# Loading K of head 0 ahead of the first wq and wo pieces in a one-token attention and MLP training step

## The chip, the cores and the metric

The kernel runs on one core of one Trainium2 chip. The metric is the device time of one execution in microseconds (us), the median of several runs. Each experiment is compared with runs of before taken in the same session, so the number for before differs a little from place to place (402.67 to 403.04). The start times in us come from the one profiled run of each kernel.

Names are those of the profile: PE is TensorE (PEld its weight loads), DVE VectorE, ACT ScalarE, POOL GpSimd, SP SyncE, and L288 is line 288 of the kernel. K0 and V0 are K and V of head 0.

## The reference, cut to what matters

One token `x` (640 wide) attends over a cache of 32 heads, each with K and V of 4096 x 128 in bf16. A small MLP runs beside it, a sigmoid gate mixes the two, and all gradients are returned, among them dK and dV, as large as the caches.

```python
x = A_x
g = _sigmoid((x * gate_w).sum(-1, keepdims=True))
a = _A_ref(x, A_k_cache, A_v_cache, A_wq, A_wo)   # softmax(q k^T) v, then @ wo
b = _B_ref(x, B_w1, B_b1, B_w2)
return g * a + (1 - g) * b
# ... and the vjp of this with grad_out
```

K and V are 67 MB together, and as much again is written as dK and dV, plus the weights and their gradients. Each byte is used for little arithmetic.

## The kernel before: the parts that matter

The bulk loads go out on the SyncE (SP) queue, in program order. Three small loads of 1.2 KB each (`vec_rows`: the rows of x, grad_out and the gate weights) go out on the ACT queue.

```python
    nc.scalar.dma_start(vec_rows[0:RC, :], x_rows)                 # L109
    nc.scalar.dma_start(vec_rows[RC:2 * RC, :], dy_rows)           # L110, grad_out
    nc.scalar.dma_start(vec_rows[2 * RC:3 * RC, :], gw_rows)       # L111, gate_w
    # ... load_k, load_v, load_wq, load_wo: one nc.sync.dma_start each
    load_wq(0)      # 1280 KB
    load_wo(0)      #  640 KB
    load_k(0)       # 1024 KB
    load_v(0)
    load_k(1)
    load_v(1)
    load_wo(1)
    # ... w1, b1, load_k(2), load_v(2), w2
```

Before the first head, a chain prepares its query and its output gradient. It starts from `vec_rows` (gate, then `da_bc`), multiplies `wo` with `da_bc` (L288, four passes), projects `x` through `wq` (L278), and ends in `x_ps` (L320). Only after these in PE's program order come the first transposes of K0:

```python
    prep_steps(0, 0)                 # qcol (wq), do_part (wo), ..., x2 -> x_ps
    for _ in range(8):
        slot(0, 9, 9)
    tk = []
    for c in range(NT):
        k_chunk(0, c, tk)            # transposes of K0 (L587)
    # ...
    for h in range(H):
        # ...
        load_k(h + 3)                # 4 K and 4 V buffers: load_k(4) waits for head 0's
        load_v(h + 3)                # last matmuls on K0 (L720)
        # ...
        period(h)
```

The loads through K3 and V3 need no buffer to come free. The load of K4 is the first that waits for compute.

Of the kernel before, what the change touches and what calls it, by code (L numbers as in the profile page):

```python
# [16 lines left out]
def kernel(  # L17
# [100 lines left out]
    def load_k(h):  # L118
        if h < H:
            kts[h] = kv_in.tile([P, J, Dh], BF16, name="Kn", tag="Kn", bufs=KB)  # L120
            nc.sync.dma_start(kts[h][:], Kv[h])

    def load_v(h):
        if h < H:
            vts[h] = kv_in.tile([P, J, Dh], BF16, name="Vn", tag="Vn", bufs=VB)
            nc.sync.dma_start(vts[h][:], Vv[h])

    def load_wq(w):
        if w < H // WG:
            wqs[w] = wts.tile([P, RC, WG * Dh], BF16, name="wq_g", tag="wq_g")  # L130
            nc.sync.dma_start(wqs[w][:], wq_v[:, :, w * WG * Dh:(w + 1) * WG * Dh])

    def load_wo(g):
        if g < NG:
            wos[g] = wts.tile([P, G, D], BF16, name="wo_g", tag="wo_g", bufs=3)
            nc.sync.dma_start(wos[g][:], wo_v[g])
# [3 lines left out]
    def load_w2(c):  # L140
        a, b = CH[c][0], min(CH[c][1], FM)
        w2cs[c] = mlp.tile([P, 5, D], BF16, name="w2c", tag="w2c", bufs=2)
        nc.sync.dma_start(w2cs[c][:, 0:b - a, :], w2_v[:, a:b, :])

    load_wq(0)
    load_wo(0)
    load_k(0)
    load_v(0)
    load_k(1)
    load_v(1)  # L150
# [711 lines left out]
```

## Time and profile before

| what | before | where it is read |
|---|---|---|
| time | 403.04 us, median of 3 runs (402.11 to 404.58) | the runs |
| span of the profiled run | 400.6 us | page, head |
| bytes moved by DMA | 164.93 MB | page, part 2 |
| rate in most slices | 415 to 428 GB/s | page, part 2 |
| busy: DVE, PE, PEld, ACT | 76%, 74%, 67%, 44% | page, part 1 |
| first transpose of K0 | 17.07 us | timeline |

These lines are part 2 of the page of before: the span in 40 equal slices of about 10 us, with the busy share of the 16 DMA engines in tenths and the rate that they moved.

```profile
DMA  8999999999999999999999999999999999999995
GB/s 288 420 415 397 421 426 417 418 423 422 425 419 424 421 422 419 419 424 422 427 415 426 422 423 419 418 428 422 421 424 423 422 421 417 423 422 416 425 378 232
DMA packets 28360, 164.93 MB, mean 412 GB/s; under 512 B 3260, under 2 KB 3964, under 8 KB 12556
```

The DMA engines are full from the second slice to the 38th. The Trainium skill, "Perfetto Trace Analysis", section Identifying the Most-Contended Engine, advises judging DMA by the HBM rate, not by occupancy. Here both say the same: about 421 GB/s in the middle, where that page (section Engine Utilization) puts the ceiling of one core's 16 engines at about 435. This trace agrees: 421 is 3% below that ceiling.

The second reading is of the start. This is the timeline of before: start in us, busy us, engine, line, operation, count, and in brackets the idle time before it with what ended it.

```profile
0.73 0.45 SPq L131 DMA_DIRECT2D wq_g<-in_A_wq_dram  x1
1.24 0.51 SPq L136 DMA_DIRECT2D wo_g<-in_A_wo_dram  x1
1.80 0.42 SPq L121 DMA_DIRECT2D Kn<-in_A_k_cache_dram  x1
...
7.04 0.17 PE L189 MATMUL cols_ps<-ident_bf,vec_rows 15*128 15x15 bf16 x1 [7.04 <-DMA vec_rows<-in_gate_w_dram]
7.09 0.33 SPq L136 DMA_DIRECT2D wo_g<-in_A_wo_dram  x1
...
11.09 0.43 ACT L229 COPY da_bc<-dab_ps 128x320 f32<-128x320 f32 x1 [2.09 <-PE dab_ps L104]
...
11.54 0.82 DVE L288 SCALAR_TENSOR_TENSOR junk<-wo_g,da_bc 128x640 bf16<-128x640 bf16 x1 [1.14 <-ACT da_bc L229]
...
17.05 0.17 PE L320 MATMUL x_ps<-m,sel 128*128 128x16 bf16 x1 [0.26 <-DVE m L315]
17.07 1.95 PE L587 MATMUL tr<-ident_f,Kn 128*128 128x128 f32 x8
```

The first transpose of K0 follows `x_ps` at once. No wait for K0 stands before it. The wait that heads the chain is the one for `vec_rows`.

### The profile page before, as it was taken

Reading aid. Unit: us, or ns where it says so; the run is one execution under the profiler, and the core shown is the slowest. Engines: PE = TensorE matmul, PEld = TensorE weight load, DVE = VectorE, ACT = ScalarE, POOL = GpSimd, SP = SyncE. Lnnn points to the kernel's source line nnn. Section 1 sums busy time; section 2 is a strip of 40 time slices with the busy share of each in tenths; the row PEclk is TensorE's granted clock in tenths of the full one; section 3 lists DMA queues with packets and bytes.
Section 4 is the critical chain, followed back from the end, with each engine's and each line's share of the span. In section 5 each row is a group of like instructions: output and inputs, shape, how many; then the busy total and the mean of one; then the engine's idle time right before and its main releaser. Section 6 shows DMA issues by size and latency. Waiting matters only on the chain.

```text
span 400.6 us, 13611 instructions
## 1 busy us (share of the span) xinstructions
PE 296.6 (74%) x5872; PEld 268.1 (67%) x5872; DVE 303.5 (76%) x791; ACT 177.1 (44%) x411; POOL 47.2 (12%) x94
## 2 busy tenths in 40 slices
PE   0688898778888788778885988819887888888200
PEld 0588787668777678668875878718776777777200
DVE  2438766646799999856688799837999997899850
ACT  1355555324554455325543555605545455545000
POOL 0001101021110111211110113101110121111000
PEclk9999999959999999959998899977999999999655
DMA  8999999999999999999999999999999999999995
GB/s 288 420 415 397 421 426 417 418 423 422 425 419 424 421 422 419 419 424 422 427 415 426 422 423 419 418 428 422 421 424 423 422 421 417 423 422 416 425 378 232
DMA packets 28360, 164.93 MB, mean 412 GB/s; under 512 B 3260, under 2 KB 3964, under 8 KB 12556
## 3 DMA queue, kind: packets, MB, share of 16 engines
q1 hardware_dynamic: 17136, 93.41, 56.5%
q0 software_dynamic: 11104, 70.64, 42.3%
q8 instruction: 46, 0.75, 0.7%
q14 instruction: 14, 0.11, 0.1%
q10 hardware_dynamic: 60, 0.01, 0.0%
HBM read 82.03 MB, written 82.03 MB: 410 GB/s over the span
## 4 chain that ended last, share of the span: by engine, by line
DVE 36%; DMA 34%; PE 17%; issue 5%; ACT 4%; SPq 0%; POOL 0%; ACTq 0%; POOLq 0%
DMA Kn<-in_A_k_cache_dram 29%; DVE dK_sb L612 9%; DVE dV_sb L612 8%; PE tr L587 7%; DVE junk L385 4%; DMA out_dram<-wo_g 4%; ACT tT L589 4%; PE sA L667 3%; DVE junk L288 3%; PE sA L596 2%; PE sB L720 2%; DVE junk L537 2%; DMA vec_rows<-in_gate_w_dram 1%; DVE wo_g L374 1%; DVE dj L707 1%
## 5 line engine op out<-in xcount | busy, mean ns | idle before, releaser
L589 ACT COPY tT<-tr 128x512 f32<-128x512 f32 x256 | 142.3, 588 | 133.9 <-PE tr L587 133.1
L596 PEld LDWEIGHTS <-tT 128*128 128x128 bf16 x2048 | 79.8, 98 | 40.1 <-ACT tT L589 34.6
L587 PE MATMUL tr<-ident_f,Kn 128*128 128x128 f32 x512 | 82.0, 298 | 9.7 <-DMA Kn<-in_A_k_cache_dram 9.7
L612 DVE TENSOR_TENSOR dV_sb<-p_bf,qd 128x2048 bf16<-128x2048 bf16 x64 | 78.0, 1218 | 0.2 <-issue 0.2
L612 DVE TENSOR_TENSOR dK_sb<-ds_bf,qd 128x2048 bf16<-128x2048 bf16 x64 | 77.7, 1216 | 0.0
L587 PE MATMUL tr<-ident_f,Vn 128*128 128x128 f32 x512 | 72.5, 277 | 0.0
L587 PEld LDWEIGHTS tr<-ident_f,Kn 128*128 128x128 f32 x512 | 61.2, 152 | 11.2 <-issue 11.2
L596 PE MATMUL sA<-qd,tT 128*128 128x48 bf16 x1024 | 48.8, 187 | 23.7 <-ACT dq_all L725 12.7
L587 PEld LDWEIGHTS tr<-ident_f,Vn 128*128 128x128 f32 x512 | 55.9, 141 | 0.0
L596 PE MATMUL sB<-qd,tT 128*128 128x48 bf16 x1024 | 46.1, 183 | 0.0
L667 PEld LDWEIGHTS <-Vn 128*128 128x128 bf16 x1024 | 30.2, 95 | 10.4 <-issue 10.4
L667 PE MATMUL sA<-e_bf,Vn 128*128 128x48 bf16 x1024 | 30.7, 183 | 7.7 <-DVE zs L687 6.1
L629 POOL DMA_DIRECT2D out_dram<-dK_sb x30 | 17.3, 576 | 138.6 <-DVE rz L689 90.6
L720 PE MATMUL sB<-ds_bf,Kn 128*128 128x48 bf16 x1024 | 32.1, 185 | 1.4 <-DVE ds_bf L709 1.4
L671 DVE TENSOR_REDUCE m<-sA 128x1 f32<-128x32 f32 x32 | 6.1, 189 | 35.2 <-PE sA L596 28.5
L720 PEld LDWEIGHTS <-Kn 128*128 128x128 bf16 x1024 | 29.4, 97 | 1.6 <-issue 1.6
L642 POOL DMA_DIRECT2D out_dram<-dV_sb x26 | 14.1, 544 | 136.8 <-DVE o_all L712 50.0
L288 DVE SCALAR_TENSOR_TENSOR junk<-wo_g,da_bc 128x640 bf16<-128x640 bf16 x32 | 26.3, 821 | 2.6 <-ACT da_bc L229 1.1
L385 DVE SCALAR_TENSOR_TENSOR junk<-wq_g,dq_bc 128x1024 bf16<-128x1024 bf16 (+1 forms) x25 | 25.1, 1005 | 0.2
L707 DVE TENSOR_SCALAR_CACHE_REDUCE dj<-sB,rz 128x128 f32<-128x128 f32 x32 | 11.1, 346 | 9.2 <-PE sB L701 9.2
L691 ACT ACTIVATE p_bf<-e_bf,rz 128x64 bf16<-128x64 bf16 x32 | 11.1, 348 | 13.6 <-DVE rz L689 10.7
L698 DVE SCALAR_TENSOR_TENSOR pj<-sB,e_bf 128x32 f32<-128x32 f32 x32 | 6.1, 190 | 12.5 <-PE sB L596 12.4
(152 smaller groups left out, 275.5 us busy)
## 6 DMA issues: line engine op xcount, KB each, us to landing
Kn<-in_A_k_cache_dram SPq DMA_DIRECT2D x32, 1024.0 KB, 23.1
Vn<-in_A_v_cache_dram SPq DMA_DIRECT2D x32, 1024.0 KB, 27.5
out_dram<-dK_sb POOLq DMA_DIRECT2D x30, 1024.0 KB, 11.7
out_dram<-dV_sb POOLq DMA_DIRECT2D x26, 1024.0 KB, 11.8
wq_g<-in_A_wq_dram SPq DMA_DIRECT2D x4, 1280.0 KB, 23.7
wo_g<-in_A_wo_dram SPq DMA_DIRECT2D x8, 640.0 KB, 16.7
out_dram<-wo_g POOLq DMA_DIRECT2D x7, 640.0 KB, 12.2
out_dram<-dwq_t SPq DMA_DIRECT2D x4, 896.0 KB, 18.3
```

The lines of the kernel that those rows point to most:

```text
L288: nc.vector.scalar_tensor_tensor(junk[:, 0:D], in0=wos[g][:, i, :], scalar=1.0, in1=da_bc[:], op0=ALU.mult, op1=ALU.mult, accum_out=gp["do ...
L385: nc.vector.scalar_tensor_tensor(junk[:, c0:c1], in0=wqs[w][:, rc, c0:c1], scalar=1.0, in1=dq_bc[:, w * WG * Dh + c0:w * WG * Dh + c1], op ...
L587: nc.tensor.transpose(tp[:, t, :], flat[:, k * P:(k + 1) * P], ident_f[:])
L589: nc.scalar.copy(sb[:].rearrange("p a b -> p (a b)"), tp[:].rearrange("p a b -> p (a b)"))
L596: nc.tensor.matmul(out[:, 2 * k:2 * k + W], lhsT=tb[:, t, par, :], rhs=vec[:, par, :].unsqueeze(1).to_broadcast([P, W // 2, 2]), start=(pa ...
L612: nc.vector.tensor_tensor(dst[:, a:b, :].rearrange("p j (a b) -> p j a b", b=2), col[:, a:b, :].unsqueeze(2).to_broadcast([P, n, Dh // 2, 2]),
L629: ring(h).dma_start(dKv[h], st["dK"][:])
L642: ring(h).dma_start(dVv[h], st["dV"][:])
L667: nc.tensor.matmul(O, lhsT=vts[h][:, j, :], rhs=st["e"][:, j:j + 1].to_broadcast([P, W]), start=(j == 0), stop=(j == J - 1))
L691: nc.scalar.activation(p_bf[:], e[:].unsqueeze(2).to_broadcast([P, J, 2]), ACT.Copy, scale=rz[:])
L707: nc.vector.tensor_scalar(dj[:], PT, rz[:], None, ALU.mult, ALU.add, accum_out=dd[:])
L720: nc.tensor.matmul(DQ, lhsT=kts[h][:, j, :], rhs=ds[:, j, 0:1].to_broadcast([P, W]), start=(j == 0), stop=(j == J - 1))
```

## The change

The intent is to have the first head's K in place earlier by loading it before the weights. Nothing else moves: the instruction streams of PE, DVE, ACT and POOL are in the same order in both kernels.

```diff
+    load_k(0)
     load_wq(0)
     load_wo(0)
-    load_k(0)
     load_v(0)
     load_k(1)
     load_v(1)
```

## The prediction

> **What bounds the kernel now.** The 16 DMA engines. The slice table shows DMA at 9 tenths in every slice but the first (8) and the last (5), and 415 to 428 GB/s in nearly every slice from the second to the 38th; 164.93 MB move in a 400.6 us span. No compute engine is near that: DVE 76%, PE 74%, PEld 67%, ACT 44%. At 421 GB/s the bytes alone need about 392 us (an estimate from those numbers), so only some 9 us are start and tail. This agrees with the Trainium skill, "Perfetto Trace Analysis", section Engine Utilization, which gives about 435 GB/s for 16 DMA engines as one core's ceiling.
>
> **What the change does.** It adds and removes nothing. On the SyncE queue the first three issues become K0, wq, wo instead of wq, wo, K0 (1024, 1280 and 640 KB); the instruction order on the other engines is identical. Whatever comes fourth starts at the same byte count.
>
> **Does the start wait for K0?** No. The chain of waits in 0 to 18 us reads: vec_rows (three small ACT-queue loads) lands at 6.9; gate and broadcasts until da_bc at 11.5; four L288 passes over wo to 15.0; d_ps, qd, dc_ps, m, x_ps to 17.2; only then, in PE program order, the first transposes of K0. K0 issues at 1.80 us and takes about 9.6 to land (11.4), over 5 us before its first use. Landing earlier buys nothing.
>
> **Does it hurt wq and wo?** From stretches of 2 us, 1.05 MB have moved by about 6.4 us, 2.36 MB by 8.8 and 3.01 MB by 10.4. So (estimates) K0 lands near 6.5, wq near 9 and wo near 10.5 to 11; they are needed at 11.3 (qcol) and 11.5 (L288). It just fits.
>
> **The side effect I expect.** vec_rows heads the chain. In the DMA packet records the grad_out and gate_w rows move only when wq is nearly drained, and wq's landing (it frees the wo(1) issue at 7.1) nearly coincides with gate_w's (6.9). With K0 and wq in front of gate_w it should land later: about 50 KB more per DMA engine at about 26 GB/s, so 1.5 us later (estimate, 0 to 2). The first K0 transpose would move from 17.1 to about 18.6 us. If grad_out and gate_w slip in behind K0 alone, the start gains up to 1 us.
>
> **How much is critical.** Almost nothing. The loads through head 3's V (14.8 MB) do not wait for compute, and only about 11 MB have moved by 30 us, when the first wait on a K buffer (L720) ends. That leaves some 8 us of backlog, so a 1.5 us later start of compute keeps the DMA engines full. PE and DVE have slack, and at about 50 to 82 us the chain waits on a K load anyway, which absorbs the lag. What remains is jitter in the tail (last two slices, 378 and 232 GB/s).
>
> **Prediction.** 403.2 us, 8 in 10 between 401.4 and 405.0. Faster by over 2%: 1.5%; within 2%: 97%; slower by over 2%: 1.5%.
>
> **What would show it.** Right: slices from the second on still about 420 GB/s; K0 landing near 6.5 us; first K0 transpose within 2 us of 17.1, released by x_ps and not by the K0 load; span within 2 us. Wrong at a step: qcol or L288 waiting on wq or wo; vec_rows landing by 6.9; a middle slice below 410 GB/s.
>
> **What would make it wrong.** The shifted completion order changing when later SyncE issues are released, so that the queue runs dry; a phase shift between loads and stores changing the tail by several us; wo landing much later than estimated; vec_rows starving for many us.

## The result, and the profile after

The changed kernel took 403.06 us (median of 6 runs, 402.36 to 404.16), before took 402.96 us (6 runs, 402.11 to 404.58). The ratio is 1.0003, with a 95% interval of 0.998 to 1.0027: the same. A ratio is the mean time of one kernel's fast runs over that of the other's of the same rounds, so it is not quite the ratio of the medians quoted.

Part 2 of the page of the changed kernel, the same lines as above:

```profile
DMA  7999999999999999999999999999999999999985
GB/s 276 422 415 404 419 425 421 419 420 423 423 421 424 421 423 417 418 426 421 422 422 422 424 425 418 418 423 421 424 423 423 425 422 420 424 418 420 425 361 215
DMA packets 28360, 164.93 MB, mean 411 GB/s; under 512 B 3260, under 2 KB 3964, under 8 KB 12556
```

The DMA picture is unchanged from the second slice to the 38th; the last two are a little lower (361 and 215 for 378 and 232). The timeline of the changed kernel's start:

```profile
0.73 0.39 SPq L121 DMA_DIRECT2D Kn<-in_A_k_cache_dram  x1
1.18 0.42 SPq L131 DMA_DIRECT2D wq_g<-in_A_wq_dram  x1
1.65 0.52 SPq L136 DMA_DIRECT2D wo_g<-in_A_wo_dram  x1
...
5.65 0.33 SPq L136 DMA_DIRECT2D wo_g<-in_A_wo_dram  x1
...
6.20 0.17 PE L189 MATMUL cols_ps<-ident_bf,vec_rows 15*128 15x15 bf16 x1 [6.20 <-DMA vec_rows<-in_gate_w_dram]
...
10.25 0.42 ACT L229 COPY da_bc<-dab_ps 128x320 f32<-128x320 f32 x1 [2.09 <-PE dab_ps L104]
...
11.48 0.82 DVE L288 SCALAR_TENSOR_TENSOR junk<-wo_g,da_bc 128x640 bf16<-128x640 bf16 x1 [1.92 <-DMA wo_g<-in_A_wo_dram]
...
16.99 0.17 PE L320 MATMUL x_ps<-m,sel 128*128 128x16 bf16 x1 [0.26 <-DVE m L315]
17.01 1.95 PE L587 MATMUL tr<-ident_f,Kn 128*128 128x128 f32 x8
```

K0 is in by about 5.6 us: the profile's waits of the SyncE queue put the issue of the second wo piece, at 5.65, behind K0's landing, as they put it behind wq's, at 7.09, before. But K0 is read first at 17.01, against 17.07 before. So it lies unused for over 11 us. Two things on the chain changed and nearly cancelled: `vec_rows` came 0.84 us earlier in this run (6.20 for 7.04), and wo, now last of the three, came so late that L288 waits for it (1.92 us idle, ended by the wo load) where it had waited for `da_bc`.

This cancelling leaves two explanations for a total that did not move. They differ in what a microsecond at the start is worth, so the experiments vary the start.

### The profile page after: what moved, and what is told of

Read it like the earlier page. It is cut to its first block, busy times and chain, and to the rows that moved or that the text cites. A ratio compares the mean times of both kernels' runs of the same rounds, so it can differ in the third digit from the quotient of the medians.

```text
span 401.4 us, 13611 instructions
## 1 busy us (share of the span) xinstructions
PE 295.7 (74%) x5872; PEld 267.4 (67%) x5872; DVE 303.5 (76%) x791; ACT 177.1 (44%) x411; POOL 47.0 (12%) x94
## 4 chain that ended last, share of the span: by engine, by line
DVE 36%; DMA 33%; PE 20%; ACT 4%; issue 2%; SPq 0%; ACTq 0%; DVEq 0%
DMA Kn<-in_A_k_cache_dram 31%; DVE dV_sb L612 9%; PE tr L587 8%; DVE dK_sb L612 8%; DVE junk L385 5%; ACT tT L589 4%; PE sA L667 3%; DVE junk L288 3%; PE sA L596 3%; DMA wo_g<-in_A_wo_dram 2%; PE sB L720 2%; DVE junk L537 2%; DVE wo_g L374 1%; DVE junk L494 1%; DVE dj L707 1%
## 5 line engine op out<-in xcount | busy, mean ns | idle before, releaser
L667 PEld LDWEIGHTS <-Vn 128*128 128x128 bf16 x1024 | 30.2, 96 | 10.5 <-issue 10.5
L288 DVE SCALAR_TENSOR_TENSOR junk<-wo_g,da_bc 128x640 bf16<-128x640 bf16 x32 | 26.3, 821 | 2.5 <-DMA wo_g<-in_A_wo_dram 1.9
## 6 DMA issues: line engine op xcount, KB each, us to landing
out_dram<-dK_sb POOLq DMA_DIRECT2D x30, 1024.0 KB, 11.4
out_dram<-wo_g POOLq DMA_DIRECT2D x7, 640.0 KB, 11.8
```

Source lines behind the costliest of these rows:

```text
L288: nc.vector.scalar_tensor_tensor(junk[:, 0:D], in0=wos[g][:, i, :], scalar=1.0, in1=da_bc[:], op0=ALU.mult, op1=ALU.mult, accum_out=gp["do ...
L667: nc.tensor.matmul(O, lhsT=vts[h][:, j, :], rhs=st["e"][:, j:j + 1].to_broadcast([P, W]), start=(j == 0), stop=(j == J - 1))
```

## The experiments

**Theory A.** The 16 DMA engines bound the kernel. The loads that need no compute (through K3 and V3) are a backlog that keeps them full until about 37 us (an estimate from their 14.8 MB and the rates), so the start of compute may move within some microseconds and cost or gain nothing.

**Theory B.** The start chain counts one for one, and the change was neutral only because an earlier `vec_rows` and a later wo cancelled.

**Rival C**, to the first half of A: the chain of compute and waits bounds the kernel, as the page's chain view may suggest (DVE 36%, DMA 34%, PE 17% for before).

### e1_pool_rows: the small rows on another queue (a miss as a test)

```diff
-    nc.scalar.dma_start(vec_rows[RC:2 * RC, :], dy_rows)
-    nc.scalar.dma_start(vec_rows[2 * RC:3 * RC, :], gw_rows)
+    nc.gpsimd.dma_start(vec_rows[RC:2 * RC, :], dy_rows)
+    nc.gpsimd.dma_start(vec_rows[2 * RC:3 * RC, :], gw_rows)
```

> Before's load order, but the grad_out and gate_w rows go out on the GpSimd queue instead of the ACT queue, ahead of everything else there. All theories: vec_rows lands by about 4 us instead of 6.9, so the first K0 transpose comes at 14 to 15 us instead of 17.1. Theory A (the DMA backlog absorbs the start): total within 0.3% of before (402 to 404 us). Theory B (the start chain counts one for one, and the change was neutral only because an earlier vec_rows and a later wo cancelled): 2 to 3 us less, about 400.3 us.

The total was 402.81 us (6 runs) against 402.67; ratio 0.9999 (0.9981 to 1.0018). But the premise failed: the rows were not early. PE had them at 8.0 us, later than before, and the first K0 transpose came at 17.98. So as a test of an earlier start it says nothing. It is one more point: a start 0.9 us later, with no cost that these runs resolve.

### e2_k_wo_wq: wo ahead of wq (a miss as a test)

```diff
-    load_wq(0)
-    load_wo(0)
     load_k(0)
+    load_wo(0)
+    load_wq(0)
```

> K0, wo, wq: as the change, with wo ahead of wq, so that wo (640 KB) is no longer the last of the three. L288 should start when da_bc is ready (10.3 to 10.7 us) and no longer wait for wo; qcol may now wait for wq until about 11.3, which is off the chain. First K0 transpose about 0.8 us earlier than in the changed kernel, at 16.1 to 16.3 us. Theory A: total within 0.3% of before. Theory B: about 0.8 us less than before, at the edge of what five rounds resolve.

Ratio 0.9997 (0.9977 to 1.0017), 402.74 us (5 runs). L288 no longer waited for wo, as expected, but `vec_rows` landed at 6.9 in this run, so `da_bc` came later and the first transpose came at 16.96, not at 16.1 to 16.3. The two theories were not told apart by this.

### e3_rows_after_v0 and e4_rows_after_v1: the start made later, in two doses

```diff
-    nc.scalar.dma_start(vec_rows[0:RC, :], x_rows)      # and the other two
     load_wq(0)
     load_wo(0)
     load_k(0)
     load_v(0)
+    nc.sync.dma_start(vec_rows[0:RC, :], x_rows)        # and the other two: e3 here,
     load_k(1)
     load_v(1)
+                                                        # e4 here instead
     load_wo(1)
```

> Before's order, with the three vec_rows loads on the SyncE queue behind V0. They land with V0, at about 4.0 MB moved, 10 to 11 us, so the first K0 transpose comes at 20 to 21 us, 3 to 4 us later than before. Theory A: within 0.3% of before. Theory B: 3 to 4 us more, about 406.5 us.

> Before's order, with the three vec_rows loads on the SyncE queue behind V1. They land at about 6.2 MB moved, 15 to 18 us; first K0 transpose 25 to 28 us, so head 0 frees its K buffer at about 38 to 41 us, where the loads that need no compute (14.8 MB) run out at about 37. Theory A: 1 to 6 us more than before, and the GB/s of the slice at 30 to 40 us below 400. Theory B: the full delay, 8 to 11 us more, about 413 us.

The first K0 transposes of e3 and of e4:

```profile
24.14 1.95 PE L587 MATMUL tr<-ident_f,Kn 128*128 128x128 f32 x8
```

```profile
28.84 1.95 PE L587 MATMUL tr<-ident_f,Kn 128*128 128x128 f32 x8
```

In e3 the delay was twice what I had expected: the first K0 transpose came at 24.14 us, 7.1 us later than before's 17.07. The total was 403.54 us (6 runs), ratio 1.0018 (0.9998 to 1.0038): about 0.7 us for 7.1 us of delay, and not clear of zero. Theory B asked for 7.

In e4 the first transpose came at 28.84 us, 11.8 us later than before, and the total was 408.34 us (4 runs), ratio 1.0137 (1.0111 to 1.0164), which is 5.5 us more. Part 2 of the page of e4 shows where it went:

```profile
DMA  8998799999999999999999999999999999999995
GB/s 294 419 416 329 267 416 414 422 425 422 418 415 422 424 421 419 419 424 422 422 423 423 422 423 421 416 425 424 422 420 427 422 421 422 413 421 419 424 396 228
```

The fourth and fifth slice fell to 329 and 267 GB/s. The stretches view of e4 (start and end in us, length, busy time of the engines, then the granted clock, the busy share of the DMA engines, and GB/s) resolves this:

```profile
35.00:37.00 2.00, 1.88 (x36) 1.69 (x35) 0.52 (x3) 1.97 (x5) 0.00 (x0) 1.00 1.01 418
37.00:39.00 2.00, 1.71 (x45) 1.60 (x45) 0.95 (x4) 0.35 (x1) 0.00 (x0) 1.00 0.90 360
39.00:41.00 2.00, 1.76 (x36) 1.51 (x35) 1.96 (x5) 1.31 (x3) 0.00 (x0) 1.00 0.05 20
41.00:43.00 2.00, 1.47 (x44) 1.35 (x40) 0.38 (x2) 1.00 (x3) 0.69 (x1) 1.00 0.31 49
43.00:45.00 2.00, 2.00 (x31) 2.00 (x32) 1.65 (x4) 1.12 (x3) 0.00 (x0) 1.00 0.79 176
45.00:47.00 2.00, 1.87 (x55) 1.69 (x54) 1.97 (x5) 1.48 (x4) 0.54 (x1) 1.00 0.99 340
```

The backlog runs out at about 38 us, and the DMA engines then have almost nothing to do until the load of K4 goes out. That is the first load that waits for compute. From 43 to 45 us the busy share (0.79) and the rate (176 GB/s) part: in the packet records the 8 KB packets of those two microseconds took 475 ns in the median, where 309 ns is usual. The timelines of the SyncE queue show its issue, in before, in e3 and in e4, in this order:

```profile
30.17 0.33 SPq L121 DMA_DIRECT2D Kn<-in_A_k_cache_dram  x1
```

```profile
36.73 0.33 SPq L118 DMA_DIRECT2D Kn<-in_A_k_cache_dram  x1
```

```profile
41.76 0.33 SPq L118 DMA_DIRECT2D Kn<-in_A_k_cache_dram  x1
```

At 30.17 and 36.73 the backlog is not yet used up; at 41.76 it is. The lost traffic accounts for the loss: summed over the five stretches from 37 to 47 us, the shortfall below 421 GB/s is 2 x (61 + 401 + 372 + 245 + 81) = 2320 KB, which is 5.5 us at 421 GB/s. The loss measured was 5.5 us. From e3 to e4 the start moved by 4.7 us and the median time by 4.8. This is theory A on both sides of its threshold.

### e9_rows_first: the start made earlier

The two delayed rows go first on the SyncE queue itself.

```diff
-    nc.scalar.dma_start(vec_rows[RC:2 * RC, :], dy_rows)
-    nc.scalar.dma_start(vec_rows[2 * RC:3 * RC, :], gw_rows)
+    nc.sync.dma_start(vec_rows[RC:2 * RC, :], dy_rows)
+    nc.sync.dma_start(vec_rows[2 * RC:3 * RC, :], gw_rows)
```

> Before's load order, with the grad_out and gate_w rows issued first on the SyncE queue, ahead of all bulk loads on that same queue (the GpSimd queue did not make them land early in e1_pool_rows). vec_rows should land at 3 to 4.5 us instead of 6.9, the bulk loads start some 0.6 us later, and the first K0 transpose comes at 14 to 15 us instead of 17.1. Theory A (backlog absorbs the start): within 0.3% of before. Theory B (start counts one for one): 2 to 3 us less, about 400.3 us.

This time the rows were early. The timeline of e9:

```profile
2.72 0.17 PE L189 MATMUL cols_ps<-ident_bf,vec_rows 15*128 15x15 bf16 x1 [2.72 <-DVE red L186]
...
9.57 0.83 DVE L288 SCALAR_TENSOR_TENSOR junk<-wo_g,da_bc 128x640 bf16<-128x640 bf16 x1 [3.49 <-DMA wo_g<-in_A_wo_dram]
...
15.10 1.95 PE L587 MATMUL tr<-ident_f,Kn 128*128 128x128 f32 x8
```

`vec_rows` is used at 2.72 us, the chain then waits for wo, and the first K0 transpose comes at 15.10, 2.0 us earlier than before. The total did not follow: 403.10 us (6 runs) against 402.90, ratio 1.0004 (0.999 to 1.0018). Theory B asked for 2 us less, a ratio of 0.995, which lies outside. Theory B falls on this side too.

The start of e9 cost something as well: it moved 254 GB/s in its first 10 us against before's 287, so 0.33 MB less, worth 0.8 us at the full rate. The interval (0.4 us less to 0.7 us more) does not show that loss. Terms below 1 us are at the edge of what these runs resolve, and I leave this one open.

### e6_drop4_dk: fewer bytes, the same arithmetic

```diff
-        elif half == 1:
+        elif half == 1 and h not in (9, 12, 15, 18):
             ring(h).dma_start(dKv[h], st["dK"][:])
```

> Wrong result on purpose: before without the dK stores of heads 9, 12, 15 and 18 (4.19 MB of 164.9 MB); every arithmetic instruction stays. Theory A (the 16 DMA engines bound the kernel): 4.19 MB at 421 GB/s, about 10 us less, 393 us. Rival C (the chain of compute and waits bounds it, as the chain view's 36% DVE and 17% PE might be read): within 2 us of before.

392.92 us (4 runs) against 402.90; ratio 0.9751 (0.9735 to 0.9766), which is 10.0 us less. The estimate from bytes was 4.19 MB / 421 GB/s = 9.96 us. The output dK was wrong, as it had to be; the other outputs agreed with the reference to within 1.4%. Rival C falls: DVE still did all its work (302.7 us busy for 303.5), but the time went down with the bytes. These are the rates of e6's page:

```profile
GB/s 288 420 416 401 423 423 418 418 420 425 424 421 426 419 402 355 420 422 421 422 424 422 423 425 413 420 423 421 426 423 421 426 420 422 421 421 418 423 421 257
```

That the two numbers agree to 0.1 us is partly luck. The 15th and 16th slice fell to 402 and 355, about 0.8 MB or 2 us short of 421, and the last two (421 and 257, for before's 378 and 232) made up for more than half of it.

### e7_k_v_wq_wo: K0 and V0 first (one look)

```diff
-    load_wq(0)
-    load_wo(0)
     load_k(0)
     load_v(0)
+    load_wq(0)
+    load_wo(0)
     load_k(1)
```

> K0, V0, wq, wo. For the small vec_rows loads: if they move only after the first bulk loads are drained, gate_w's row comes after V0, at 7.5 to 8 us, and vec_rows lands at about 8. If they move at some 5.3 to 6 us whatever bulk is ahead of them (as in before, the change and e2_k_wo_wq), vec_rows lands at 6 to 7. wo lands at about 4 MB moved, 12 to 13 us; L288 waits for it and the first K0 transpose comes at 18 to 19 us. Total (one look): within 0.5% of before by theory A.

One run gave 403.03 us. L288 waited for wo until 13.67, and the first K0 transpose came at 19.21, 2.1 us later than before, at no cost that one run would show. `vec_rows` was used at 6.71, so the small rows did not wait for V0.

### e10_tail_pool: can theory A find a faster version?

If only DMA time counts, the place to look is where the DMA engines are not full. One such place is the tail. Before issued its last two stores, of dwo and dwq, late; the waits of the SyncE queue show 9.8 us behind the landing of a dV store and then 2.0 us behind one of dwq:

```profile
376.40 3.31 SPq L627 DMA_DIRECT2D out_dram<-dK_sb  x2
389.53 0.33 SPq L375 DMA_DIRECT2D out_dram<-wo_g  x1
391.90 0.38 SPq L793 DMA_DIRECT2D out_dram<-dwq_l  x1
```

The changed kernel, with one edit more:

```diff
-            (nc.sync if g == NG - 1 else nc.gpsimd).dma_start(dwo_v[g], wos[g][:])
+            nc.gpsimd.dma_start(dwo_v[g], wos[g][:])
-    nc.sync.dma_start(dwq_v[:, :, CL:], dwq_l[:])
+    nc.gpsimd.dma_start(dwq_v[:, :, CL:], dwq_l[:])
```

> The changed kernel, with the last dwo store and the last dwq store issued on the GpSimd queue instead of the SyncE queue, where before issued them at 389.5 and 391.9 us although their data were ready at 379.9 and 381.2 (a completion counter to be reused held them back). They should go out at about 380 and 381.5. Theory A says that time when the DMA engines are not full is what counts, and the stretch of 386 to 393 us moves some 0.6 MB less than 420 GB/s would: 1 to 2.5 us less than before, about 401 us. If that dip isn't the end's limit: no difference.

The stores went out at 380.64 and 381.96 us, as expected (in the changed kernel, from which e10 starts, at 390.37 and 392.77):

```profile
380.64 0.61 POOL L375 DMA_DIRECT2D out_dram<-wo_g  x1 [18.18 <-DVE wo_g L374]
381.96 0.90 POOL L793 DMA_DIRECT2D out_dram<-dwq_l  x1 [0.70 <-DVE ambj L803]
```

The stretches of the tail, first before, then e10 (columns as above):

```profile
384.00:388.00 4.00, 0.27 (x1) 0.09 (x1) 2.53 (x9) 0.26 (x1) 0.00 (x0) 0.50 0.94 394
388.00:392.00 4.00, 0.00 (x0) 0.00 (x0) 0.00 (x0) 0.00 (x0) 0.00 (x0) 0.50 0.81 336
392.00:396.00 4.00, 0.00 (x0) 0.00 (x0) 0.00 (x0) 0.00 (x0) 0.00 (x0) 0.50 0.83 321
396.00:400.00 4.00, 0.00 (x0) 0.00 (x0) 0.00 (x0) 0.00 (x0) 0.00 (x0) 0.50 0.31 114
```

```profile
384.00:388.00 4.00, 0.28 (x1) 0.09 (x1) 2.98 (x11) 0.26 (x1) 0.00 (x0) 0.50 1.01 424
388.00:392.00 4.00, 0.00 (x0) 0.00 (x0) 0.00 (x0) 0.00 (x0) 0.00 (x0) 0.50 0.93 380
392.00:396.00 4.00, 0.00 (x0) 0.00 (x0) 0.00 (x0) 0.00 (x0) 0.00 (x0) 0.50 0.63 259
396.00:400.00 4.00, 0.00 (x0) 0.00 (x0) 0.00 (x0) 0.00 (x0) 0.00 (x0) 0.50 0.28 116
```

The dip at 384 to 392 filled up, but then the rate fell sooner, and the last packet ended at 399.4 us (399.1 in before, 399.9 in the changed kernel). The total was 402.62 us (6 runs) against 402.90; ratio 0.999 (0.9977 to 1.0004), not a gain clear of noise. So my expectation of 1 to 2.5 us was wrong, and theory A in the plain form "total bytes over total rate" does not hold for the tail. From 392 us on, a busy share of 0.63 and then 0.28 means that some of the 16 DMA engines were done while others still had work. The packet records of the trace bear this out: in e10 the number of packets in flight (of 256 B or more, median over each microsecond) stays at 16 until 390 us, is 11 from 392, 10 from 393 and 7 from 397. In before it is already 11 from 388 to 390 us, while the two stores wait to be issued. So the backlog is uneven. That the earlier stores gave work only to the engines that were ahead, and so gained nothing, is my reading; it is argued, not shown, since the records do not say which engine moved a packet.

### The start against the total

| kernel | first K0 transpose, us | shift from before, us | ratio (95% interval) |
|---|---|---|---|
| e9_rows_first | 15.10 | -2.0 | 1.0004 (0.999 to 1.0018) |
| the change | 17.01 | -0.1 | 1.0003 (0.998 to 1.0027) |
| e1_pool_rows | 17.98 | +0.9 | 0.9999 (0.9981 to 1.0018) |
| e3_rows_after_v0 | 24.14 | +7.1 | 1.0018 (0.9998 to 1.0038) |
| e4_rows_after_v1 | 28.84 | +11.8 | 1.0137 (1.0111 to 1.0164) |

Over 9 us of shift the total stays within 0.2%. Past the end of the backlog, where e4 is the only point, it rises with about the full excess.

## Why the prediction was right, point by point

- **The kernel is bound by the DMA engines: right, and shown.** Taking away 4.19 MB took 10.0 us (e6); starving the DMA engines of 2.3 MB of traffic cost 5.5 us (e4). By these runs alone the limit could as well be a memory that all engines share. The packet records of the tail speak against that: in e10 a packet of 4 KB took 159 ns in the median with 16 to 18 in flight and the same 159 with 1 to 4, and one of 7 KB 272 ns with 16 to 18 and with 9 to 12. When engines fall idle, the others get no faster.
- **Nothing waits for K0: right.** Both timelines show the first transposes directly behind `x_ps`. K0 landed at about 5.6 us, where "near 6.5" was predicted.
- **wq and wo "just fit": half wrong.** wo landed at about 11.4, a little later than the 10.5 to 11 estimated, and `da_bc` was ready sooner than I assumed, so L288 waited for wo. It is one of the signs that the prediction named for "wrong at a step". It cost the start nothing net, and the total nothing that shows.
- **The wait on a K load "at about 50 to 82 us [...] absorbs the lag": right.** In e3 the loads of K4 to K8 go out about 6.6 us later than in before (36.73 for 30.17, and at the end 77.68 for 71.10), that of K9 0.9 us later (89.07 for 88.18) and, after one straggler (K10, 5.2 us later), those of K11 and K12 0.2 us later (120.20 for 120.00). In e4 the load of K12 is still 5.2 us late (125.21), about what e4 lost.
- **The side effect on `vec_rows`: wrong.** The step was "With K0 and wq in front of gate_w it should land later: [...] so 1.5 us later". It landed 0.84 us earlier in the profiled run. I had read a dependence on the bulk bytes ahead out of one trace where gate_w's landing happened to coincide with wq's. In the profiled runs with unchanged small loads, PE used `vec_rows` at 7.04 and 6.62 us with before's order (before, e6) and at 6.20 and 6.67 with the changed order (after, e10). With K0, wo, wq it was 6.9 (e2), and with K0, V0 first 6.71 (e7). So the order of the bulk loads has no effect on it that these runs resolve; two runs of one order differ by half a microsecond. The predicted 18.6 us for the first transpose fell with it (17.01). The prediction had named the other outcome too ("If grad_out and gate_w slip in behind K0 alone, the start gains up to 1 us"); the rows did come earlier, but L288's wait for wo took the gain. That the start moved by only 0.06 us is luck: two errors cancelled. The total does not rest on it.
- **"some 8 us of backlog": right in size.** 7.1 us of delay cost about 0.7 us (not clear of zero), 11.8 us cost 5.5 us. Of the 11.8 us, 11.8 - 5.5 = 6.3 us were free, and of the 7.1 us 6.4, so the free part is 6 to 7 us.
- **A sign that I had chosen badly.** "A middle slice below 410 GB/s" was to show the prediction wrong. The fourth slice was at 397 in before already, and at 404 after.

What stays open: why the small rows on the ACT queue move as late as they do (next section), and which engines hold the longer backlog in the last 10 us of the tail, and why.

## What to carry to other kernels

Before moving a load forward, look for a wait on it: a load that nothing waits for can't gain, and moving it ahead of others can turn one of those into the new wait. In a kernel whose DMA engines are full, ask how much already-issued traffic stands between the engines and the first load that needs compute; within that backlog the start of compute is free in both directions, and beyond it (one case here, e4) each microsecond counts. A mechanism read out of two landings that coincide in one trace needs a second trace.

## What the Trainium skill lacked or had wrong

- "DMA: Bandwidth & Descriptors", section Queues, rings and completion order, says that each DMA engine takes turns between the queues that it has work for, a packet of some 9 to 17 descriptors at a time. One record of wq (2 KB) took 84 ns in these traces and one of K (8 KB) 309, so, if a record is a descriptor and a packet of these loads holds that many, which no run shows, a turn of wq would take 0.8 to 1.4 us and one of K 2.8 to 5.3 (estimates from the page's count). A small load on its own queue would then wait longer behind K than behind wq. Here the packets of the grad_out and gate_w rows, issued on the ACT queue at 1.3 to 2.0 us, moved only at about 4.9 to 6.3 us (before, after, e2, e6, e7, e10), and on the GpSimd queue, issued at 1.3 to 2.5 us, at 5.6 to 7.3 (e1), while x's row, first on the ACT queue, moved mostly at 1.7 us. Issued first on the SyncE queue, ahead of the bulk, the same rows moved at 1.7 to 2.3 us (e9). The delay was about the same with wq first (before) and with K0 first (after). The page does not explain that, and no run here shows the cause.
- The same page, section Issuing engines are not separate DMA queues, says that DMAs of all issuing engines interleave on the same 16 engines and that spreading them saves only issue time. The runs agree in the total: the two stores of the tail, issued 9 to 10 us sooner on the GpSimd queue, gained 0.1% with an interval that includes zero. What the section does not say is that the choice of queue can delay a small load by microseconds: PE used the rows at 7.04 us with the ACT queue and at 7.95 with the GpSimd queue, where their packets moved late though nothing bulky stood ahead of them on that queue, and at 2.72 us when they went first on the SyncE queue.
- I found no page that says how the end of a DMA-bound kernel drains. Here the DMA engines' mean busy share fell from 1.01 to 0.63 and 0.28 over the last 15 us although the two late stores were already queued (e10). The packets in flight fell from 16 to 10 and then 7, so some engines end earlier than others. A per-engine number on each packet record would be needed to say which, and why.
